# Query chunks, half key tiles and output rows laid out as contiguous pieces in an attention and top-k kernel

## The chip, the core and the metric

One core of a Trainium2 chip runs the kernel; the other seven are idle. The metric is device time in microseconds of one execution, the median of several runs, lower is better. The engines are TensorE (PE, with its weight loads as PEld), VectorE (DVE), ScalarE (ACT), GpSimd (POOL) and SyncE (SP), which issues every load, store and DMA transpose of the main loop.

## What is computed

For each of four batches: keys and values are the 4 x 4 mean of `kv`, projected with `w_sr`; 12288 queries of 128 channels attend to 768 keys; then the 128 rows with the highest score `x @ w_gate` pass through a small MLP and are written back.

```python
kv_pool = kv.reshape(B, H // r, r, W // r, r, C).mean(axis=(2, 4))
k = v = kv_pool.reshape(B, -1, C) @ w_sr
s = scale * (q @ k.transpose(0, 2, 1))
a = np.exp(s - s.max(-1, keepdims=True)); a /= a.sum(-1, keepdims=True) + 1e-09
x = a @ v
top_idx = np.argpartition(-scores[b], capacity)[:capacity]     # scores = x @ w_gate
out[b, top_idx] = x[b, top_idx] + sigmoid(scores[top_idx])[:, None] * (relu(xe @ w1) @ w2)
```

## The kernel before

The work is cut into 192 blocks of 256 queries (`BLK`), 48 for each batch. For block i TensorE makes 2 x 128 x 768 scores in PSUM (`S`, three products of split operands), VectorE takes the row maximum (`s_max`, tile `m`, one instruction in each block), ScalarE the exponential (`exp`, tile `am`). The weights are split into an fp16 high part (ScalarE) and a bf16 low part (GpSimd, for most of it), tile `hl`, and `turn` transposes each part with one DMA transpose (`at<-hl`, 128 x 11 x 128 of two bytes). Four blocks later (`LAG`) `AV` multiplies the transposed weights with the values into `o_two`. VectorE divides, and `finish` collects `GROUP` blocks in tile `x` before a store goes to `out`.

Queries come in chunks of `CHUNK` columns, 128 channels on the partitions. `load_q` (L138) loads half a chunk of 2048 at a time, which is 1024 columns or 512 KB, into one of two buffers; `split_q` (L356) reads it on ScalarE and GpSimd two blocks at a time. In the array `in_q` (L848) one channel's data of all batches and chunks follow each other, so a channel's rows lie 4 x 12288 x 4 B = 192 KiB apart and each load reads 128 pieces of 4 KB. Keys are loaded by `load_kv` (L126) in six tiles for each batch, most of them as two halves of 512 KB, for the first batch at the start and for the next batch while the blocks of this one run (`next_keys`, L298). `in_kv` (L849) has the same 192 KiB between channels. Pooling of the next keys runs on GpSimd. An output tile holds 2048 rows as 16 rows for each partition, of which a store (L476) writes eight: 4 KB out of every 8 KB.

The order on the four compute engines is the order of the code (`InOrder`). SP isn't held to that: its transfers are ordered by a scheduler, and an SP instruction that waits holds all that stand behind it. Transfers take eight semaphores in turn, so each also waits for the one eight before it.

Of the kernel before, what the change touches and what calls it, by code (L numbers as in the profile page):

```python
# [19 lines left out]
P = 128  # L20
B, N, C = 4, 12288, 128
HK, WK, R = 384, 32, 4
M = (HK // R) * (WK // R)
KT = M // P
TAPS = R * R
CHUNK = 2048
JPC = CHUNK // P
NCH = N // CHUNK
QT = 2
BLK = QT * P  # L30
NBLK = N // BLK
BPC = CHUNK // BLK
VC = C + 2
NCOL = N // P
CUT = 2 * M - P
GROUP = 4
OWN = 256
SHARE = CUT - OWN
ORDER = (2, 3, 4, 0, 1, 5)
# [32 lines left out]
def attention_topk_mlp(ctx, tc, a, outs, capacity):  # L72
    nc = tc.nc
# [4 lines left out]
    kvp = ctx.enter_context(tc.tile_pool(name="kvp", bufs=3))  # L78
    kvs = ctx.enter_context(tc.tile_pool(name="kvs", bufs=2))
    keys = ctx.enter_context(tc.tile_pool(name="keys", bufs=2))  # L80
    qp = ctx.enter_context(tc.tile_pool(name="qp", bufs=2))
    qs = ctx.enter_context(tc.tile_pool(name="qs", bufs=3))
    wk = ctx.enter_context(tc.tile_pool(name="wk", bufs=3))
    hlp = ctx.enter_context(tc.tile_pool(name="hlp", bufs=4))
# [41 lines left out]
    def load_kv(b, kc, parts=1, t=None):  # L126
        late = t is not None
        if not late:
            t = kvp.tile([P, 2, P // 2, TAPS], F32, name="kv_raw")
        n = 2 // abs(parts)  # L130
        for i in range(abs(parts)):
            if parts > 0 or late == (i > 0):
                nc.sync.dma_start(out=t[:, i * n:(i + 1) * n], in_=a["kv"][:, b, kc, i * n:(i + 1) * n])
        return t

    qraw = {}

    def load_q(b, ch, lo=0, hi=CHUNK):  # L138
        if (b, ch) not in qraw:
            qraw[b, ch] = qp.tile([P, CHUNK], F32, name="q_raw")  # L140
        nc.sync.dma_start(out=qraw[b, ch][:, lo:hi], in_=a["q"][:, b, ch, lo:hi])

    kvset = {}

# [77 lines left out]
    def first_keys():  # L222
# [3 lines left out]
        nc.sync.dma_start(out=cst, in_=a["cst"])  # L226
        raws += [load_kv(0, kc, 2) for kc in range(3, KT)]
        load_q(0, 0, 2 * BLK, CHUNK)
        split_q(0, 0)
        kv = kvset[0]  # L230
        for kc in range(KT):
# [124 lines left out]
    def split_q(b, blk):  # L356
        ch, h = divmod(blk, BPC)
        raw = qraw[b, ch][:, h * BLK:(h + 2) * BLK]
        qh = qs.tile([P, 2 * BLK], F32R, name="qh")
        ql = qs.tile([P, 2 * BLK], BF16, name="ql")  # L360
        act.copy(qh, raw)
        pool.tensor_tensor(out=ql, in0=raw, in1=qh.bitcast(F32), op=ALU.subtract)
        for i in range(2):
            h = qh[:, i * BLK:(i + 1) * BLK]
            top = h.bitcast(BF16).rearrange("p (n h) -> p n h", h=2)[:, :, 1]
            qsplit[b, blk + i] = h, top, ql[:, i * BLK:(i + 1) * BLK]
# [96 lines left out]
    def finish(n):  # L463
        b, blk = blocks[n]
        o, rz = st[n]["o"], st[n]["rz"]
        if blk % GROUP == 0:
            xt_[b] = ob.tile([P, GROUP * QT, C], F32, name="x")
        x = xt_[b]
        if b not in scores:
            scores[b] = tk.tile([P, NCOL], F32, name="sc")  # L470
        if n < nb - 2:
            dve.tensor_tensor(out=scores[b][:, blk * QT:(blk + 1) * QT], in0=o[:, :, C + 1], in1=rz, op=ALU.mult)
        dve.tensor_tensor(out=x[:, (blk % GROUP) * QT:(blk % GROUP + 1) * QT], in0=o[:, :, 0:C], in1=rz.rearrange("p (j o) -> p j o", o=1).broadcast_to([P, QT, C]), op=ALU.mult)
        if blk % GROUP == GROUP - 1:
            ch, h = divmod(blk // GROUP, BPC // GROUP)
            nc.sync.dma_start(out=outs[b].rearrange("(h p j) d -> h p j d", p=P, j=JPC)[ch, :, h * GROUP * QT:(h + 1) * GROUP * QT], in_=x)  # L476
        del st[n]

    def topk(b):
# [189 lines left out]
    for i in range(nb):  # L669
        m = i - LAG + (i < TURN)  # L670
        old = m >= 0 and i != TURN
        b, blk = blocks[i]
        if blk % GROUP == 0 and i + BPC < nb:
            nb_, nblk = blocks[i + BPC]
            load_q(nb_, nblk // BPC, nblk % BPC * BLK, (nblk % BPC + GROUP) * BLK)
        if blk == 0 and b + 1 < B:
            start(prep, next_keys(b + 1))
        if i:
# [183 lines left out]
```

## Time and profile before

| | |
|---|---|
| runs of the kernel before | 980.07, 983.41, 985.01 us, median 983.41 us |
| the profiled execution | 981.31 us; its span 979.5 us |
| granted TensorE clock, mean | 0.971 |
| moved by DMA | 217.61 MB, mean 222 GB/s |
| transposes, query loads, half key tiles, stores | 384, 46, 36, 48 |

The span is the time from the first to the last instruction; the execution's own time is 1.8 us longer. All times in rows are microseconds from the span's start, if nothing else is said. A busy TensorE isn't TensorE at its best, since matmuls overlap; a DMA share over 1 means that packets of one engine overlap.

### The profile page before, as it was taken

The page shows a single profiled execution, that of the slowest core. Times are in us where ns is not written, and L with a number is a line of the kernel's source. Part 1 is how long each engine was busy: PE and PEld are TensorE (multiplying, and loading weights), DVE is VectorE, ACT ScalarE, POOL GpSimd, SP SyncE. Part 2 cuts the span into 40 slices and gives each one's busy share as a digit, 9 for nine tenths or more (in the row PEclk, how much of TensorE's full clock was granted, in tenths as well). Part 3 has the DMA queues.
Part 4 walks back from the last instruction along what each step waited for, and adds up shares of the span by engine and source line. Part 5 has one row for each costly group of instructions (what it writes and reads, how often), then busy time and mean ns, then how long its engine had stood idle before and what let it go on. Part 6 is the DMA issues. An engine that isn't in the chain of part 4 may idle for free.

```text
span 979.5 us, 26075 instructions
## 1 busy us (share of the span) xinstructions
PE 895.3 (91%) x9797; PEld 718.0 (73%) x9971; DVE 752.7 (77%) x2120; ACT 748.0 (76%) x1361; POOL 691.3 (71%) x487
## 2 busy tenths in 40 slices
PE   4899898999999899899999989999999999999954
PEld 3577777777777787787777767877787877877743
DVE  6767676676788788688777768888868888888874
ACT  3688687787988788788888768888888888888700
POOL 2587677776787878788778778888767766667500
PEclk9999999999999999999999999999999999999966
DMA  9899999999999999999999999999989999999910
GB/s 360 225 237 218 226 239 249 239 229 232 253 225 224 239 263 229 234 249 248 224 213 233 216 248 263 223 227 220 226 172 229 226 241 222 231 216 189 206 37 6
DMA packets 574687, 217.61 MB, mean 222 GB/s; under 512 B 555360, under 2 KB 556512, under 8 KB 573792
## 3 DMA queue, kind: packets, MB, share of 16 engines
q1 hardware_dynamic: 574304, 215.41, 104.8%
q8 instruction: 78, 1.28, 0.6%
q0 software_dynamic: 256, 0.52, 0.2%
q14 instruction: 49, 0.40, 0.1%
HBM read 52.04 MB, written 25.43 MB: 79 GB/s over the span
## 4 chain that ended last, share of the span: by engine, by line
PE 54%; DMA 13%; issue 10%; DVE 9%; POOL 7%; ACT 6%; POOLq 0%; SPq 0%; DVEq 0%; ACTq 0%
PE s L57 29%; PE o_two L57 25%; DMA at<-hl 12%; DVE m L57 3%; ACT am L57 3%; POOL hl L57 3%; POOL ql L57 2%; POOL kv_sum L57 2%; ACT hl L57 2%; DVE junk L57 1%; DMA kv_raw<-in_kv 1%; DVE pooled L57 1%; ACT s L57 1%; DVE hl L57 0%; DVE mg L57 0%
## 5 line engine op out<-in xcount | busy, mean ns | idle before, releaser
L57 POOL TENSOR_TENSOR hl<-am,hl 128x1152 bf16<-128x1152 f32 x191 | 453.9, 2377 | 216.4 <-ACT hl L57 109.2
L57 PE MATMUL o_two<-vx,at 128*128 128x130 f16 x6804 | 438.6, 221 | 26.8 <-DMA at<-hl 26.2
L57 PEld LDWEIGHTS <-at 128*128 128x128 f16 (+1 forms) x6912 | 402.5, 97 | 82.5 <-issue 46.5
L57 DVE TENSOR_REDUCE m<-s 128x2 f32<-128x1536 f32 x192 | 337.3, 1757 | 112.8 <-PE s L57 112.4
L57 ACT ACTIVATE am<-s,m 128x512 f32<-128x512 f32 (+1 forms) x384 | 306.3, 798 | 100.8 <-DVE m L57 99.0
L57 PE MATMUL s<-kh,qh 128*128 128x512 f32 (+1 forms) x768 | 362.6, 474 | 0.0
L57 PE MATMUL s<-kb,ql 128*128 128x256 bf16 (+1 forms) x705 | 227.6, 323 | 7.2 <-issue 0.7
L57 ACT CAST hl<-am 128x1152 f16<-128x1152 f32 x192 | 225.3, 1173 | 0.0
L57 PE MATMUL s<-kl,qh 128*128 128x256 bf16 (+1 forms) x657 | 213.0, 324 | 1.3 <-DVE mg L57 0.5
L57 PEld LDWEIGHTS s<-kh,qh 128*128 128x128 f32 x768 | 146.9, 191 | 50.5 <-issue 1.7
L57 POOL TENSOR_TENSOR ql<-q_raw,qh 128x512 bf16<-128x512 f32 x96 | 122.7, 1278 | 6.2 <-ACT qh L57 6.2
L57 PEld LDWEIGHTS <-qh 128*128 128x128 bf16 x768 | 83.5, 109 | 22.7 <-issue 5.4
L57 ACT ACTIVATE s<-s,m 128x256 f32<-128x256 f32 x192 | 86.0, 448 | 6.3
L57 PEld LDWEIGHTS <-ql 128*128 128x128 bf16 x768 | 75.9, 99 | 5.9 <-issue 1.8
L57 DVE TENSOR_TENSOR hl<-s,hl 128x256 bf16<-128x256 f32 x192 | 79.5, 414 | 0.1
L57 DVE TENSOR_TENSOR x<-o_two,rz 128x256 f32<-128x256 f32 x189 | 78.3, 414 | 0.0
L57 ACT CAST at<-s 128x128 f16<-128x128 f32 x192 | 50.9, 265 | 34.2 <-PE s L57 33.9
L57 DVE TENSOR_TENSOR at<-s,at 128x128 bf16<-128x128 f32 x192 | 54.8, 285 | 22.5 <-ACT at L57 19.1
L57 ACT CAST hl<-s 128x256 f16<-128x256 f32 x191 | 71.1, 372 | 0.0
L57 PE MATMUL s<-cst,am 128*128 128x128 f32 x192 | 61.2, 319 | 8.1 <-ACT am L57 7.7
L57 PEld LDWEIGHTS s<-cst,am 128*128 128x128 f32 x192 | 26.9, 140 | 54.9 <-ACT am L57 52.8
L57 DVE TENSOR_SCALAR rz<-o_two,sg 128x2 f32<-128x2 f32 x189 | 40.9, 216 | 29.0 <-PE o_two L57 27.9
(171 smaller groups left out, 632.4 us busy)
## 6 DMA issues: line engine op xcount, KB each, us to landing
out<-x SPq DMA_DIRECT2D x48, 512.0 KB, 3.8
q_raw<-in_q SPq DMA_DIRECT2D x46, 512.0 KB, 5.1
kv_raw<-in_kv SPq DMA_DIRECT2D x36, 512.0 KB, 4.9
kv_raw<-in_kv SPq DMA_DIRECT2D x6, 1024.0 KB, 9.2
at<-hl SPq DMA_TRANSPOSE x384, 4.3
w<-in_w SPq DMA_DIRECT2D x2, 512.0 KB, 8.6
q_raw<-in_q SPq DMA_DIRECT2D x1, 768.0 KB, 7.1
cst<-in_cst SPq DMA_DIRECT2D x1, 320.0 KB, 9.7
```

The source lines that it names most:

```text
L57: r = f(*args, **kwargs)
```

## The change

Both input arrays get another order in memory: `in_q` is now batch, chunk, channel, column with `CHUNK` = 1024, and `in_kv` is batch, tile, half, channel, key, so what one load reads (1024 columns of 128 channels, or half a key tile) is one stretch of 512 KB, still 4 KB for each partition. A whole key tile is read as two such stretches, with pieces of 4 KB where 8 KB stood. The chunk of 1024 queries is 128 partitions of eight rows each, so the four blocks of one store are one stretch of 512 KB too. There are four query buffers of half the size, and one load fills one of them; in the code it stands eight blocks (`AHEAD`) before its use, as before. At the start the second part of the first chunk and the second chunk are two loads. The numbers that turn a position in a tile into a row of `out` follow `CHUNK`.

```diff
-CHUNK = 2048
+CHUNK = 1024
...
-GROUP = 4
+GROUP = BPC
+AHEAD = 2 * BPC
...
-    qp = ctx.enter_context(tc.tile_pool(name="qp", bufs=2))
+    qp = ctx.enter_context(tc.tile_pool(name="qp", bufs=4))
...
-                nc.sync.dma_start(out=t[:, i * n:(i + 1) * n], in_=a["kv"][:, b, kc, i * n:(i + 1) * n])
+                nc.sync.dma_start(out=t[:, i * n:(i + 1) * n], in_=a["kv"][b, kc, i * n:(i + 1) * n].rearrange("h c k t -> c h k t"))
...
-        nc.sync.dma_start(out=qraw[b, ch][:, lo:hi], in_=a["q"][:, b, ch, lo:hi])
+        nc.sync.dma_start(out=qraw[b, ch][:, lo:hi], in_=a["q"][b, ch, :, lo:hi])
...
         load_q(0, 0, 2 * BLK, CHUNK)
+        load_q(0, 1)
...
-            ch, h = divmod(blk // GROUP, BPC // GROUP)
-            nc.sync.dma_start(out=outs[b].rearrange("(h p j) d -> h p j d", p=P, j=JPC)[ch, :, h * GROUP * QT:(h + 1) * GROUP * QT], in_=x)
+            nc.sync.dma_start(out=outs[b].rearrange("(h p j) d -> h p j d", p=P, j=JPC)[blk // GROUP], in_=x)
...
-        if blk % GROUP == 0 and i + BPC < nb:
-            nb_, nblk = blocks[i + BPC]
-            load_q(nb_, nblk // BPC, nblk % BPC * BLK, (nblk % BPC + GROUP) * BLK)
+        if blk % GROUP == 0 and i + AHEAD < nb:
+            nb_, nblk = blocks[i + AHEAD]
+            load_q(nb_, nblk // BPC)
...
-        "q": np.ascontiguousarray(q.reshape(B, NCH, P, JPC, C).transpose(4, 0, 1, 3, 2).reshape(C, B, NCH, CHUNK)),
-        "kv": np.ascontiguousarray(kv.reshape(B, KT, 2, HK // R // KT // 2, R, WK // R, R, C).transpose(7, 0, 1, 2, 3, 5, 4, 6).reshape(C, B, KT, 2, P // 2, TAPS)),
+        "q": np.ascontiguousarray(q.reshape(B, NCH, P, JPC, C).transpose(0, 1, 4, 3, 2).reshape(B, NCH, C, CHUNK)),
+        "kv": np.ascontiguousarray(kv.reshape(B, KT, 2, HK // R // KT // 2, R, WK // R, R, C).transpose(0, 1, 2, 7, 3, 5, 4, 6).reshape(B, KT, 2, C, P // 2, TAPS)),
```

The sequences of TensorE, VectorE, ScalarE and GpSimd stay what they were. SP's changes in where the loads stand. Its first place is in the third batch, in the trace of before from 548 to 575 us. Names ending in a number are one buffer's use; an `x2` behind a transpose is a block's high and low part. Before:

```order
L133 DMA kv_raw_9491<-in_kv 128x1024
L476 DMA out_2<-x_8508 128x1024
L440 DMA_TRANSPOSE at_8727<-hl_8726 128x11x128 x2
L141 DMA q_raw_9086<-in_q 128x1024
L440 DMA_TRANSPOSE at_8810<-hl_8809 128x11x128 x2
L141 DMA q_raw_9086<-in_q 128x1024
L440 DMA_TRANSPOSE at_8888<-hl_8887 128x11x128
L133 DMA kv_raw_9491<-in_kv 128x1024
L440 DMA_TRANSPOSE at_8888<-hl_8887 128x11x128
L440 DMA_TRANSPOSE at_8973<-hl_8972 128x11x128 x2
L476 DMA out_2<-x_8828 128x1024
```

And the same place on SP now:

```order
L134 DMA kv_raw_9508<-in_kv 128x1024
L477 DMA out_2<-x_8523 128x1024
L442 DMA_TRANSPOSE at_8742<-hl_8741 128x11x128 x2
L142 DMA q_raw_9424<-in_q 128x1024
L442 DMA_TRANSPOSE at_8826<-hl_8825 128x11x128 x2
L134 DMA kv_raw_9508<-in_kv 128x1024
L442 DMA_TRANSPOSE at_8904<-hl_8903 128x11x128 x2
L442 DMA_TRANSPOSE at_8989<-hl_8988 128x11x128 x2
L477 DMA out_2<-x_8844 128x1024
L442 DMA_TRANSPOSE at_9071<-hl_9070 128x11x128 x2
L142 DMA q_raw_9746<-in_q 128x1024
```

The second query load has moved from beside the first to four blocks behind it, and no longer stands ahead of the half key tile. The second place on SP is in the last batch, where no keys are loaded. Before:

```order
L476 DMA out_3<-x_12401 128x1024
L440 DMA_TRANSPOSE at_12616<-hl_12615 128x11x128 x2
L141 DMA q_raw_12957<-in_q 128x1024 x2
L440 DMA_TRANSPOSE at_12698<-hl_12697 128x11x128 x2
L440 DMA_TRANSPOSE at_12775<-hl_12774 128x11x128 x2
```

Now:

```order
L477 DMA out_3<-x_12422 128x1024
L442 DMA_TRANSPOSE at_12637<-hl_12636 128x11x128 x2
L142 DMA q_raw_13295<-in_q 128x1024
L442 DMA_TRANSPOSE at_12720<-hl_12719 128x11x128 x2
L442 DMA_TRANSPOSE at_12797<-hl_12796 128x11x128 x2
L442 DMA_TRANSPOSE at_12877<-hl_12876 128x11x128 x2
L477 DMA out_3<-x_12738 128x1024
L442 DMA_TRANSPOSE at_12953<-hl_12952 128x11x128 x2
L142 DMA q_raw_13604<-in_q 128x1024
```

Two loads behind each other, once in eight blocks, have become one load in every four. SP's wait on GpSimd, which stood at the first of the two, now stands at each from the sixth chunk on.

## Rows read from the trace of the kernel before

**Rows 1.** The page: busy time, share of the span and instructions of each engine, and the mean busy share of the DMA engines in 40 slices (tenths).

```profile
PE 895.3 (91%) x9797; PEld 718.0 (73%) x9971; DVE 752.7 (77%) x2120; ACT 748.0 (76%) x1361; POOL 691.3 (71%) x487
...
DMA  9899999999999999999999999999989999999910
```

**Rows 2.** The chain of waits from 848 to 880 us, in order of time: start, us, what. `s` are scores, `o_two` the products with values.

```profile
852.65 2.23 PE s L57 x12
854.88 1.05 PE o_two L57 x18
...
855.93 1.05 PE o_two L57 x18
856.98 2.23 PE s L57 x12
```

**Rows 3.** Instructions on tile `m`, the row maximum: duration in ns min/median/max, first and last start.

```profile
L57 DVE TENSOR_REDUCE m<-s x192: 1742/1757/1759, 25.6 to 921.4; 128x2 f32<-128x1536 f32 x192
```

**Rows 4.** What TensorE waited for from 25.6 to 925.7 us, its matmuls in the first row and its weight loads in the second: us in total, times, longest.

```profile
PE o_two L57 <- DMA at<-hl: 26.2, 30, 3.8
...
PEld L57 <- DMA at<-hl: 35.2, 35, 3.9
```

**Rows 5.** What TensorE's matmuls waited for from 746 to 925.7 us, all rows.

```profile
PE s L57 <- ACT am L57: 1.0, 2, 0.6
PE o_two L57 <- DVE x L57: 0.4, 2, 0.3
PE s L57 <- DVE hl L57: 0.3, 1, 0.3
```

**Rows 6.** Stretches of the first, third and last batch: start to end, length, busy time of PE, PEld, DVE, ACT and POOL (instructions), granted clock, DMA share, GB/s. The stretches below have the same columns.

```profile
25.60:260.00 234.40, 213.96 (x2292) 168.57 (x2328) 163.64 (x361) 181.45 (x326) 173.88 (x122) 0.98 1.13 233
...
485.10:712.10 227.00, 216.54 (x2412) 174.32 (x2455) 181.51 (x510) 187.61 (x344) 180.83 (x131) 0.99 1.11 228
712.10:925.70 213.60, 210.31 (x2389) 168.70 (x2431) 175.25 (x484) 182.23 (x328) 147.00 (x82) 1.00 1.05 214
```

**Rows 7.** The first and the last of five such stretches (the others begin at 223.4, 339.4 and 397.5 us).

```profile
110.70:114.10 3.40, 3.40 (x25) 2.78 (x24) 0.88 (x4) 0.00 (x0) 1.56 (x2) 0.51 1.30 228
...
571.50:574.90 3.40, 2.93 (x27) 2.88 (x28) 0.96 (x6) 0.00 (x0) 0.37 (x1) 0.51 1.17 330
```

**Rows 8.** TensorE in order of time ahead of those two stretches: start, us, instruction, and in brackets the idle time before it with what ended it.

```profile
109.15 0.86 PE L57 MATMUL o_two<-vx,at 128*128 128x130 f16 x12 [1.97 <-DMA at<-hl]
...
571.75 0.83 PE L57 MATMUL o_two<-vx,at 128*128 128x130 f16 x6 [3.75 <-DMA at<-hl]
```

**Rows 9.** DMA issues: count, KB each, median us from issue to landing.

```profile
q_raw<-in_q SPq DMA_DIRECT2D x46, 512.0 KB, 5.1
kv_raw<-in_kv SPq DMA_DIRECT2D x36, 512.0 KB, 4.9
...
at<-hl SPq DMA_TRANSPOSE x384, 4.3
```

**Rows 10.** Stretches through one query load that was issued at 136.4 us between transposes: the transposes ahead of it, its first and second microsecond, its end, the transposes behind it.

```profile
136.60:137.40 0.80, 0.75 (x8) 0.59 (x7) 0.42 (x4) 0.74 (x2) 0.80 (x2) 1.00 1.28 288
137.60:138.60 1.00, 1.00 (x10) 0.78 (x8) 0.59 (x2) 0.87 (x2) 0.76 (x1) 1.00 1.25 164
138.60:139.60 1.00, 1.00 (x16) 0.75 (x15) 0.51 (x1) 1.00 (x3) 0.00 (x0) 1.00 0.76 168
139.60:140.20 0.60, 0.60 (x14) 0.60 (x12) 0.60 (x1) 0.51 (x1) 0.01 (x1) 1.00 0.96 353
140.20:141.00 0.80, 0.80 (x18) 0.80 (x16) 0.80 (x2) 0.05 (x1) 0.80 (x1) 1.00 1.41 185
```

**Rows 11.** Stretches from a load's first byte until transposes run at their rate again: that query load alone, then two pairs of query loads; the last row is a store, first to last byte.

```profile
137.40:141.10 3.70, 3.70 (x48) 3.16 (x47) 2.79 (x5) 2.53 (x5) 1.88 (x2) 1.00 1.08 204
...
175.40:180.50 5.10, 5.02 (x55) 3.99 (x56) 3.90 (x10) 4.19 (x10) 5.01 (x6) 1.00 1.05 235
...
808.30:812.90 4.60, 4.55 (x56) 3.71 (x55) 4.15 (x13) 4.08 (x8) 2.65 (x2) 1.00 1.05 262
...
246.60:247.80 1.20, 1.20 (x23) 1.19 (x21) 1.20 (x1) 0.80 (x1) 1.20 (x2) 1.00 1.10 408
```

**Rows 12.** Stretches at the kernel's start, before any transpose: `w_sr` (64 KB, contiguous), the first query piece (2 KB for each channel), whole key tiles (8 KB pieces), half key tiles and query pieces.

```profile
2.00:2.20 0.20, 0.00 (x0) 0.00 (x0) 0.00 (x0) 0.02 (x1) 0.00 (x0) 1.00 0.56 159
2.20:2.80 0.60, 0.00 (x0) 0.00 (x0) 0.00 (x0) 0.22 (x1) 0.00 (x0) 1.00 0.81 119
4.00:9.00 5.00, 0.00 (x0) 0.00 (x0) 2.04 (x2) 0.59 (x1) 1.25 (x1) 1.00 0.99 406
12.00:20.00 8.00, 6.67 (x43) 5.83 (x44) 7.81 (x8) 2.61 (x9) 2.66 (x8) 1.00 1.02 407
```

**Rows 13.** SP in order of time: start, us that the issue took with its waits, instruction.

```profile
554.83 1.49 SPq L141 DMA_DIRECT2D q_raw<-in_q  x1
...
560.46 0.56 SPq L141 DMA_DIRECT2D q_raw<-in_q  x1
...
562.56 0.58 SPq L133 DMA_DIRECT2D kv_raw<-in_kv  x1
563.24 8.71 SPq L440 DMA_TRANSPOSE at<-hl  x3
```

**Rows 14.** What SP waited for at query loads: us in total, times, longest.

```profile
SPq L141 <- POOL ql L57: 4.1, 4, 1.7
...
SPq L141 <- POOL pooled L57: 2.6, 2, 1.5
```

## The prediction

> **What bounds the kernel now.** I read the page first: TensorE is busy 91% of the span and the DMA engines are at 0.9 or more in nearly every slice [rows 1]. Two resources are near their limit, so the question is which of them ends a block. In the chain of waits the late blocks show it: twelve score matmul records (2.23 us) and two groups of value products (1.05 us each) follow each other with nothing between, and a block starts every 4.33 us (852.65 to 856.98) [rows 2]. That is TensorE's floor. The row-maximum instruction runs once per block, first at 25.6 and last at 921.4 us [rows 3]: 895.8 us for 191 steps, where the floor is 191 x 4.33 = 827.0. So 68.8 us of the main loop are lost.
>
> Next I asked what TensorE waited for in the loop. The one large item that isn't its own issue or a short wait on ScalarE is the DMA transpose `at<-hl`: 26.2 us seen by the matmuls, 35.2 us seen by the weight loads, up to 3.9 us at once [rows 4]. In the last 180 us before the tail, where no keys are loaded, no DMA wait is left at all [rows 5]. The stretches say the same: the first batch has DMA share 1.13 and TensorE busy 213.96 of 234.40 us, the last 1.05 and 210.31 of 213.60 [rows 6]. A long wait costs a second time: just after five of them the granted clock is 0.50 to 0.51 for 3.4 us, which is 1.2 instead of 2.4 GHz, after a stretch in which TensorE sat idle [rows 7, 8]. Half of 5 x 3.4 us is 8.5 us. DMA therefore costs the loop 26.2 + 8.5 = 34.7 to 35.2 + 8.5 = 43.7 us; I take the middle, 39. The other 30 us have other causes (the start, short waits on ScalarE) and aren't touched.
>
> **Why transposes are late.** All transfers go through SP's queue in order. A transpose lands 4.3 us after its issue in the median, a query load 5.1, a half key tile 4.9 [rows 9]. The rate during one query load tells why: transposes before it move 288 GB/s, the first two microseconds of the load 164 and 168, its end 353, and the transposes that follow start at 185 [rows 10]. From its first byte until transposes run freely again the single load takes 3.7 us; two in a row take 4.6 to 5.1, so 2.3 to 2.6 each. A store of the same size moves 408 GB/s and takes 1.3 us [rows 11]. The same strided loads, streaming at the kernel's start with no transposes, reach 406 to 407 GB/s, or 524,288 B / 407 = 1.29 us for 512 KB [rows 12]. So the pieces 192 KiB apart aren't slow in a stream; their onset is. One pair of rows bears on the cause: the first transfer of all (`w_sr`, contiguous) moves 159 GB/s at a DMA share of 0.56, the strided query piece behind it 119 at a share of 0.81 [rows 12]. Per busy share that is 284 against 147 GB/s, although the contiguous one has pieces of only 512 B.
>
> Per four blocks (17.3 us at the floor) the engines owe: eight transposes of 128 x 1408 x 2 B = 360,448 B at 288 GB/s, 1.25 us each, 10.0; one store, 1.3; one query load, 2.3 to 2.6 as half of a pair; and in the first three batches one half key tile (12 in 48 blocks), 2.3 to 3.7. Together 15.9 to 17.6 us of 17.3 with keys, 13.6 to 13.9 without. The first waits and the second doesn't [rows 4, 5]: the queue is just full.
>
> **The change, part by part.** *Contiguous loads.* If the onset goes, a load costs between 1.29 us and what it costs now; I take 1.5, near the streaming rate, because the contiguous first transfer shows no slow onset. Four blocks then owe 10.0 + 1.3 + 1.5 + 1.5 = 14.3 us, near the last batch's 13.6 to 13.9, which has no DMA wait. Of 39 us I let 5 stay, for stages where keys and queries still come together, and none to all of it as the bounds. *Single query loads.* The order shows one load per eight transposes in place of two per sixteen, so around 549 to 572 us, where SP now issues query, query and key tile within 8 us and one transpose group then takes 8.71 us [rows 13], one of the three is gone. That only helps, by an amount that is inside the 39. *Waits.* Every query load from the sixth chunk on now waits for GpSimd to leave its buffer, where every second one did. Such waits cost SP 4.1 and 2.6 us in 4 and 2 places [rows 14]; twice that is 7 us more, with the transposes queued behind. A block's transposes are read four blocks later, so I cost it at nothing (0 to 2 us); without that slack it would be the 7 us. *Stores* already move at full rate [rows 11]: 0. *Key tiles loaded whole* go from pieces of 8 KB to 4 KB: 406 and 407 GB/s are the two rates, 0 [rows 12]. *The start*: the slow 0.6 us at 119 instead of 406 GB/s could give back 0.4 us [rows 12]; 0 to 0.4, left out. The order of the instructions on the four compute engines doesn't change.
>
> Sum: 39 - 5 = 34 us off the profiled execution (981.31 us, its span 979.5), so 947; off the median of the runs (983.41), 949. What is late next is TensorE itself, at its 4.33 us a block [rows 2].
>
> **The rivals.** *B: the layout doesn't matter, the onset stays.* For it: strided pieces stream at full rate [rows 12], so memory can serve them, and the onset may belong to any read behind transposes; no row shows a contiguous read there. Then pairs become singles, which shortens the bursts but pays the onset twice. I take the two as even: 983 us, 978 to 988. The Trainium skill, DMA: Bandwidth & Descriptors, section Latency and other measured facts, says that copies lose rate only when the rows of a tile lie 2 MiB or more apart, and keep it at 512 KiB; it advises contiguous tiles beyond. By that rule 192 KiB costs nothing and B is the outcome; the trace agrees for the stream and speaks against it for the onset, which the rule doesn't tell of.
>
> *D: slower.* Same mechanism, but the second onset outweighs the shorter bursts. A query load goes from 2.4 to 3.7 us; 36 of them lie in the three batches with keys, 47 us more DMA time. Today 72 loads there cost 1.0 to 2.4 us above streaming, about 120 us, and 39 of it reaches TensorE, a third. A third of 47 is 15 us, less some relief from the shorter bursts: 994 us. It decides at 2.4 us: a single contiguous load that holds the engines for longer makes the kernel slower, for less makes it faster.
>
> *The change does less than it says*: the onset shrinks to half. Loads at 2.2 us give 15.7 us per four blocks, below the 15.9 to 17.6 of now; two thirds of the 34 would still come, 961. I count it with the forecast.
>
> **How the numbers follow.** Forecast 0.68, at 949 (941 to 963: all 43 us gone to only half the onset gone). B 0.20 at 983. D 0.12 at 994. A measurement of this kernel can tell about 0.5% (4.9 us) from no change. Faster than that: the forecast and a little of B, 0.72. Within: most of B, some of D, 0.16. Slower: 0.12. The range 940 to 985 holds the forecast and more than half of B, about 0.8; the forecast's own range is 941 to 963.
>
> **What would show it.** Right: single loads that hold the engines for 1.3 to 2 us, at over 300 GB/s from the first microsecond; a landing time of query loads under 4.5 us; `at<-hl` waits of TensorE under 10 us where they were 26.2 and 35.2; no half-clock stretch after the first; the first three batches within 3% of the last one's pace. Wrong: the same 150 to 200 GB/s at onset (B or D), or DMA waits gone and their time back as waits on GpSimd or ScalarE.

## The result, and the profile after

The changed kernel takes 994.73 us (median of 6 runs, 991.79 to 1000.32), the kernel before in the same session 982.72 (6 runs, 976.43 to 986.55): ratio 1.0134, 95% interval 1.009 to 1.0177. It is slower by 12.0 us, where 34 us less were forecast. The profiled execution took 996.49 us, its span is 994.7. Three executions of the runs below (one of e6, two of e7) took over 1.5% longer than the fastest of the same kernel, 1003.06 to 1014.43 us, and are left out of the tables.

The page: TensorE's row and the busy share of the DMA engines. Both stand as in [rows 1].

```profile
PE 900.9 (91%) x9797; PEld 722.9 (73%) x9971; DVE 752.2 (76%) x2120; ACT 748.8 (75%) x1361; POOL 691.9 (70%) x487
...
DMA  9899999999999999999999999999999999999910
```

The row maximum, which answers to [rows 3]: it starts 1.0 us later, and its 191 steps take 936.8 - 26.6 = 910.2 us where they took 895.8. Nearly the whole loss lies in the loop.

```profile
L58 DVE TENSOR_REDUCE m<-s x192: 1743/1758/1760, 26.6 to 936.8; 128x2 f32<-128x1536 f32 x192
```

What TensorE's matmuls waited for from 26.6 to 941 us, then its weight loads (two answers of the same view). In [rows 4] the transposes stood at 26.2 and 35.2; now they cost 38.0 and 51.4, in more but shorter waits. One execution is a small sample here: e14 and e15 below run as fast as the kernel before and show 31.5 / 43.5 and 32.2 / 43.9.

```profile
PE o_two L58 <- DMA at<-hl: 38.0, 39, 2.7
PE s L58 <- ACT am L58: 6.5, 10, 3.1
...
PEld L58 <- DMA at<-hl: 51.4, 54, 2.8
```

The four batches (columns as in [rows 6]). The first three are 5.3, 4.3 and 4.7 us longer than before (239.70 against 234.40, 229.40 against the 225.1 from 260.0 to 485.1 us, 231.70 against 227.00); the last takes 213.60 as it did. Look at the last column too: 225 to 232 GB/s wherever keys are loaded, at a DMA share well over 1. The first row is the second batch before, which [rows 6] leave out.

```profile
260.00:485.10 225.10, 214.66 (x2381) 172.02 (x2424) 181.66 (x508) 186.20 (x341) 179.52 (x129) 0.98 1.17 240
...
26.60:266.30 239.70, 215.66 (x2292) 170.60 (x2328) 164.02 (x361) 181.72 (x326) 173.91 (x122) 0.97 1.13 228
266.30:495.70 229.40, 213.96 (x2376) 170.87 (x2418) 181.53 (x507) 186.51 (x340) 179.78 (x129) 0.99 1.15 232
495.70:727.40 231.70, 219.30 (x2410) 176.82 (x2457) 180.62 (x509) 187.67 (x344) 180.93 (x131) 0.98 1.15 225
727.40:941.00 213.60, 210.33 (x2388) 168.69 (x2431) 175.22 (x484) 182.31 (x328) 147.18 (x82) 1.00 1.08 214
```

The DMA issues, median landing time last. In [rows 9] queries stood at 5.1, half key tiles at 4.9 and transposes at 4.3; neither kind of load lands sooner, and transposes land later. The six whole key tiles do land sooner (7.4 us against 9.2), the stores later (4.5 against 3.8).

```profile
q_raw<-in_q SPq DMA_DIRECT2D x47, 512.0 KB, 5.1
kv_raw<-in_kv SPq DMA_DIRECT2D x36, 512.0 KB, 5.1
...
at<-hl SPq DMA_TRANSPOSE x384, 4.6
```

Stretches through one contiguous query load, as [rows 10] showed a strided one: transposes at 292 GB/s ahead of it, then 71 and 115 in its first two microseconds, 334 at its end. The slow onset is still there. The last row is one of seven stretches of the loop at clock 0.50, 1.2 GHz, each just behind a wait for transposes; before there were five [rows 7].

```profile
256.20:257.00 0.80, 0.80 (x7) 0.40 (x6) 0.52 (x4) 0.80 (x3) 0.00 (x0) 1.00 1.61 292
257.00:258.00 1.00, 1.00 (x20) 1.00 (x20) 0.89 (x1) 1.00 (x3) 0.00 (x0) 1.00 1.26 71
258.00:259.00 1.00, 1.00 (x21) 1.00 (x19) 1.00 (x2) 0.66 (x3) 0.82 (x1) 1.00 0.32 115
259.00:260.00 1.00, 1.00 (x8) 0.54 (x7) 0.93 (x5) 0.97 (x2) 1.00 (x1) 1.00 0.98 334
260.00:261.00 1.00, 1.00 (x10) 0.78 (x7) 0.76 (x3) 1.00 (x3) 1.00 (x2) 1.00 1.16 207
...
610.60:614.00 3.40, 3.18 (x20) 2.60 (x19) 1.46 (x8) 1.73 (x5) 0.17 (x1) 0.50 1.15 195
```

### The profile page after: what moved, and what is told of

It reads as the page before. It is cut to its first block, busy times and chain, and to the rows that moved or that the text cites. A ratio compares the mean times of both kernels' runs of the same rounds, so it can differ in the third digit from the quotient of the medians.

```text
span 994.7 us, 26096 instructions
## 1 busy us (share of the span) xinstructions
PE 900.9 (91%) x9797; PEld 722.9 (73%) x9971; DVE 752.2 (76%) x2120; ACT 748.8 (75%) x1361; POOL 691.9 (70%) x487
## 4 chain that ended last, share of the span: by engine, by line
PE 50%; DMA 18%; issue 9%; DVE 9%; POOL 6%; ACT 6%; POOLq 0%; SPq 0%; DVEq 0%; ACTq 0%
PE s L58 27%; PE o_two L58 23%; DMA at<-hl 17%; DVE m L58 4%; ACT am L58 3%; POOL hl L58 2%; POOL kv_sum L58 2%; POOL ql L58 2%; ACT hl L58 1%; DMA kv_raw<-in_kv 1%; DVE junk L58 1%; ACT s L58 1%; DVE pooled L58 0%; DVE idx L58 0%; DVE mg L58 0%
## 5 line engine op out<-in xcount | busy, mean ns | idle before, releaser
L58 PEld LDWEIGHTS <-at 128*128 128x128 f16 (+1 forms) x6912 | 403.4, 98 | 96.3 <-DMA at<-hl 51.4
L58 ACT ACTIVATE am<-s,m 128x512 f32<-128x512 f32 (+1 forms) x384 | 306.4, 798 | 99.4 <-DVE m L58 98.5
L58 PEld LDWEIGHTS s<-cst,am 128*128 128x128 f32 x192 | 26.9, 140 | 51.7 <-ACT am L58 49.6
```

What stands on the lines that cost most here:

```text
L58: r = f(*args, **kwargs)
```

## The experiments

Each table gives the median, its runs and the ratio to the kernel before, which ran beside it on the same chip (984.7 to 986.2 us in the five sessions). The at<-hl column holds the waits of matmuls / weight loads on the transposes in the one profiled execution of each; before it was 26.2 / 35.2. In the cuts of code, `...` stands for what is left out.

### Layout or single loads?

`e1_layout_only` takes the contiguous layout alone: query loads still come in pairs into two large buffers, rows are stored as before.

```
-... in_=a["q"][:, b, ch, lo:hi])
+... in_=a["q"][b, ch, h, :, lo - h * HALF:hi - h * HALF])
...
-... in_=a["kv"][:, b, kc, i * n:(i + 1) * n])
+... in_=a["kv"][b, kc, i * n:(i + 1) * n].rearrange("h c k t -> c h k t"))
...
```

> The kernel before with the new order in memory alone: query half chunks and half key tiles contiguous, still two buffers of 2048 columns, so two query loads stand together once in eight blocks; stores as before. Onset theory (the first microseconds of a load behind transposes are slow whatever the layout, and single loads pay it twice as often): 983 us, 978 to 988, TensorE's wait on the transposes 26 us as before. Layout theory (contiguous pieces 16 KiB apart for neighbouring engines are slower to start than pieces 192 KiB apart): 990 to 995, waits near the 38 us of the changed kernel.

`e2_single_only` keeps the strided layout and takes four half buffers, so that query loads come one by one.

```
-qp = ctx.enter_context(tc.tile_pool(name="qp", bufs=2))
+qp = ctx.enter_context(tc.tile_pool(name="qp", bufs=4))
...
-    qraw[b, ch] = qp.tile([P, CHUNK], F32, name="q_raw")
+    qraw[b, ch, h] = qp.tile([P, HALF], F32, name="q_raw")
...
```

> The kernel before with single loads alone: four buffers of 1024 columns, so one query load stands in every four blocks; order in memory strided as before, stores as before. Onset theory: 992 to 998 us, waits on the transposes near 38 us. Layout theory: 983 us, since nothing in memory moved; with shorter bursts perhaps 978.

`e4_after_paired` is the changed kernel with two chunks in one buffer again, so that its loads pair up; loads and stores stay contiguous.

```
-qp = ctx.enter_context(tc.tile_pool(name="qp", bufs=4))
+qp = ctx.enter_context(tc.tile_pool(name="qp", bufs=2))
...
-    qraw[b, ch] = qp.tile([P, CHUNK], F32, name="q_raw")
+    qraw[b, pair] = qp.tile([P, 2, CHUNK], F32, name="q_raw")
...
```

> The changed kernel (contiguous loads and stores) with two chunks in one buffer, so that its query loads stand in pairs again. Onset theory: back to 983 us, 978 to 988. Layout theory: stays at 990 to 995. A loss that came from contiguous stores: stays at 990 to 995 while the layout of the loads alone costs nothing.

| kernel | us | lowest to highest | ratio, interval | at<-hl |
|---|---|---|---|---|
| layout alone (e1) | 991.23 | 986.99 to 995.77 | 1.0053, 1.0029 to 1.0076 | 35.9 / 47.5 |
| single loads alone (e2) | 987.79 | 983.09 to 992.36 | 1.0019, 0.9988 to 1.005 | 31.9 / 44.9 |
| after, paired (e4) | 991.89 | 986.32 to 994.73 | 1.0062, 1.0033 to 1.009 | 35.5 / 46.9 |

Neither half of the change gains. The layout costs 0.3 to 0.8%, as the layout theory had said of e1 and e4. With strided loads it isn't shown that single loads cost anything by themselves, since the interval of e2 includes 1; its 987.8 us fit neither theory (992 to 998, or 983). On top of the contiguous layout they do seem to cost: e1 and e4, which keep the pairs, are at 1.0053 and 1.0062, the changed kernel at 1.0134, its interval (1.009 to 1.0177) above that of e1 and meeting that of e4 at its edge; they come from two sessions, so this is a hint. e4 and e1 agree, so no gain or loss from contiguous stores shows. The medians of e1 and e2 add up to 6.4 + 3.0 = 9.4 of the 12.0 us.

### What a load costs among transposes

`m1_onset` holds transfers alone, in rows of repetitions: four transposes of the kernel's size, then one transfer of 512 KB.

```
+for i in range(16):
+    turns(4)
+    t = ld.tile([P, HALF], F32, name=name)
+    nc.sync.dma_start(out=t, in_=what(i))
```

> No part of the reference is computed: only transfers on one queue, in sections of 64 transposes with sixteen 512 KB transfers among them. Transposes alone take 1.25 us each, 5.0 us for four. Onset theory: four transposes and one load take 8.0 to 8.7 us, strided and contiguous alike; eight and a pair 14.6 to 15.1; a 1 MB load costs one onset like a pair; a copy inside SBUF or a store has no onset, 6.3 us; a load right behind a store has less of it, because the reading side can run ahead while the store is written. Layout theory: strided and contiguous singles differ by over 0.5 us each.

SP in order of time (start, us of the issue, instruction): first and last issue of a row of strided loads, of contiguous ones (`whole`), of strided pairs behind eight transposes each, of copies from SBUF (`inside`), of stores, then 64 transposes with nothing between.

```profile
51.11 0.92 SPq L51 DMA_DIRECT2D strided<-in_qs  x1
...
163.13 0.90 SPq L51 DMA_DIRECT2D strided<-in_qs  x1
...
171.79 0.90 SPq L51 DMA_DIRECT2D whole<-in_qc  x1
...
300.42 0.92 SPq L51 DMA_DIRECT2D whole<-in_qc  x1
...
316.02 1.26 SPq L58 DMA_DIRECT2D strided<-in_qs  x2
...
434.98 1.23 SPq L58 DMA_DIRECT2D strided<-in_qs  x2
...
580.25 0.78 SPq L68 DMA_DIRECT2D inside<-src  x1
...
705.85 0.76 SPq L68 DMA_DIRECT2D inside<-src  x1
...
714.24 0.80 SPq L71 DMA_DIRECT2D out<-src  x1
...
840.68 0.81 SPq L71 DMA_DIRECT2D out<-src  x1
841.54 110.16 SPq L33 DMA_TRANSPOSE at<-hl  x64
```

A transpose takes 110.16 / 64 = 1.72 us, not the 1.25 us of the prediction. A repetition takes (163.13 - 51.11) / 13 = 8.62 us with a strided load, (300.42 - 171.79) / 15 = 8.58 with a contiguous one, (705.85 - 580.25) / 15 = 8.37 with a copy from SBUF, and (840.68 - 714.24) / 15 = 8.43 with a store. Less 4 x 1.72 = 6.88 that leaves 1.74, 1.70, 1.49 and 1.55 us. Strided pairs take (434.98 - 316.02) / 7 = 16.99 us a repetition, contiguous pairs 16.87: 1.6 us a load, so a pair saves 0.1 to 0.15 us on each. A load of 1 MB takes 3.3 us, as much as a pair, and a load right behind a store isn't cheaper (3.4 us for both).

Stretches through one contiguous load of m1 (length, busy time of VectorE and GpSimd, clock, DMA share, GB/s): the transposes ahead of it, its first two microseconds, the transposes behind it.

```profile
257.00:259.00 2.00, 0.00 (x0) 0.00 (x0) 1.00 1.11 211
259.00:260.00 1.00, 0.00 (x0) 0.00 (x0) 1.00 0.75 147
260.00:261.00 1.00, 0.00 (x0) 0.00 (x0) 1.00 0.85 283
262.00:264.00 2.00, 0.00 (x0) 0.00 (x0) 1.00 1.27 265
```

The onset is there too, but the transposes behind the load then move 265 GB/s where those ahead of it moved 211: part of what the onset loses comes back. So in a full queue the slow onset costs at most some 0.25 us over a copy from SBUF, which has none (355 GB/s from 640.5 to 641.5 us), and the layout makes no difference. The layout theory (over 0.5 us a load) is out, and of the onset theory the 1.25 us of a transpose and the 6.3 us for a repetition with a copy or a store.

Four blocks with a key load then owe 8 x 1.72 + 1.55 + 2 x 1.74 = 18.8 us, or 226 a batch. That is the 225.1 and 227.00 us that the second and third batch took before [rows 6]; the first took 234.40, 8 us more, which stays unexplained. Without keys it is 17.05, or 205, under TensorE's 209.4 (209.3 in the last batch, 712.1 to 921.4 us). Theory T, for the runs that follow: the 16 DMA engines are full in batches 0 to 2. The expectations below count with a rougher split of the same rows, 1.6 us for a transpose and 2.0 us for any transfer of 512 KB, which adds up to the same 18.8.

### One queue, or the engines behind it?

`e5_after_kv_on_act` and `e6_before_kv_on_act` issue the loop's key loads from ScalarE's queue, `e7_after_q_on_act` the query loads.

```
e5 and e6
-nc.sync.dma_start(out=t[:, i * n:(i + 1) * n], in_=a["kv"]...
+(nc.sync if b == 0 else act).dma_start(out=t[:, i * n:(i + 1) * n], in_=a["kv"]...
e7
-nc.sync.dma_start(out=qraw[b, ch][:, lo:hi], in_=a["q"]...
+(nc.sync if (b, ch) < (0, 2) else act).dma_start(out=qraw[b, ch][:, lo:hi], in_=a["q"]...
```

> The changed kernel with the key and value loads of the loop (36 half tiles and whole tiles of batches 1 to 3) issued by ACT, so that they leave SP's queue; layout, query loads, stores and transposes stay. Theory Q (one queue in order is the bound of batches 0 to 2): by the run with transfers alone, a transpose takes 1.6 us of SP's queue and a 512 KB transfer behind it 2.0 us, so four blocks need 8 x 1.6 + 3 x 2.0 = 18.8 us, against 17.45 us that four blocks of the last batch take; without the key load 8 x 1.6 + 2 x 2.0 = 16.8 us fit, the batches fall from 239.7, 229.4 and 231.7 us to 210 to 220 each, waits of the matmuls on at<-hl from 38 us to under 10, and the time to 930 to 955 us. Theory E (the 16 DMA engines themselves are the bound, whatever queue feeds them): the same bytes at the same price, 985 to 1000 us. Rival: the load on its own queue takes the engines from a transpose that is due, and the issue costs ACT time: 1000 to 1015 us.

> The kernel before with the key and value loads of the loop issued by ACT, all else as before (strided pieces, query loads in pairs). Theory Q: batches 0 to 2 from 234.5, 225.0 and 227.0 us to 210 to 220, time 930 to 950 us. Theory E: 978 to 988 us. If the layout costs the same with the keys on their own queue, this one is 3 to 8 us faster than the changed kernel with the same edit; if the layout only counts where the queue is full, the two are within 2 us.

> The changed kernel with the query loads issued by ACT (all but the first two chunks), key loads on SP's queue. Theory Q: the same room as with the keys moved, in batches 0 to 2: 930 to 955 us; the last batch stays at 209 us, since its queue had room already. Theory E: 985 to 1000 us.

| kernel | us | lowest to highest | ratio, interval |
|---|---|---|---|
| after, keys by ScalarE (e5) | 997.87 | 988.23 to 999.33 | 1.0101, 1.0039 to 1.0163 |
| before, keys by ScalarE (e6) | 997.71 | 991.07 to 999.63 | 1.0112, 1.0062 to 1.0163 |
| after, queries by ScalarE (e7) | two runs | 986.88 and 988.21 | none |

The DMA queues of e5 (packets, MB, share of 16 engines):

```profile
q1 hardware_dynamic: 570080, 196.53, 100.4%
q10 hardware_dynamic: 5136, 18.88, 7.0%
```

What its matmuls waited for from 25.6 to 935 us, the largest row:

```profile
PE o_two L58 <- DMA at<-hl: 36.6, 30, 3.8
```

The key loads (18.88 MB) went over a queue of their own, and TensorE still waits 36.6 us for transposes that stand in another. A single queue in order isn't what delays them: theory Q falls, and E, the engines, stands. Whether it is the engines themselves or the memory behind them that is full, these runs don't tell apart. e7 gave no interval; its two runs lie in theory E's range of 985 to 1000 us, far from the 930 to 955 of theory Q.

`m2_engines_or_queue` asks the same with transfers alone.

```
+turns(4)
...
+nc.scalar.dma_start(out=t, in_=strided(i))
...
+turns(2)
+loads(1, "strided1", strided, nc.sync)
...
+turns(2)
+loads(1, "whole1", whole, nc.sync)
```

> Transfers alone, nothing of the reference is computed: rows of 16 repetitions of four DMA transposes on SP with one strided 512 KB load on ACT's queue beside them; 48 transposes issued by SP and ACT in turn; 24 strided and 24 contiguous loads with no transposes; rows of two transposes and one load, strided and contiguous. Theory T (engines): four transposes with the load beside them take 8.4 to 8.6 us as in one queue; transposes from two queues 1.5 to 1.6 us each; loads alone 1.3 to 1.6 us; two transposes and a load 3.2 + 2.0 = 5.2 us in either layout. Theory Q (SP's issue sets the pace): 6.5 us with the load beside, and 1.25 us or less for each of the transposes from two queues. A dearer contiguous load would show in the loads alone or in the row with two transposes, by more than 0.05 us a load.

SP in order of time: 128 transposes, in whose first part ScalarE's queue brought 16 loads; the second and the last of the rows with two transposes and one load (strided, then the first and last contiguous one). The last line is the only wait of SP on a transfer in the first of these stretches (us, times, longest).

```profile
3.20 249.92 SPq L33 DMA_TRANSPOSE at<-hl  x128
...
545.75 0.52 SPq L69 DMA_DIRECT2D strided<-in_qs  x1
...
608.11 0.53 SPq L69 DMA_DIRECT2D strided<-in_qs  x1
...
613.11 0.58 SPq L69 DMA_DIRECT2D whole<-in_qc  x1
...
691.00 0.53 SPq L69 DMA_DIRECT2D whole<-in_qc  x1
...
SPq L33 <- DMA at<-hl: 5.8, 1, 5.8
```

At 1.72 us, 128 transposes take 220.2 us. Of the other 29.7 us SP stood 5.8 at the end, when ScalarE's own transposes had begun (248.29 us). That leaves 23.9 us: 1.5 us for each of the 16 loads of the other queue, or 1.3 if two loads that SP had issued itself just before (0.74 us) are counted with them. They cost nearly what they cost in line. The rows give (608.11 - 545.75) / 12 = 5.20 us strided and (691.00 - 613.11) / 15 = 5.19 contiguous, 1.76 and 1.75 us a load, so neither layout is dearer. Two of the rows planned don't bear: the scheduler put all 16 of ScalarE's loads at the start, so that no period could be read there, and mixed strided with contiguous loads in the rows without transposes. Nor does the row with transposes from two queues: SP waited 130.0 us there for transposes to land, and 48 of them took 164.7 us.

### Are the engines full?

`e9_after_no_keys` leaves the loop's key loads out, `e10_single_strided_twice` and `e11_after_twice` issue each query load twice.

```
e9
+    fixed = []
...
+        if b:
+            return fixed[0]
...
e10 and e11
...
-    ob = ctx.enter_context(tc.tile_pool(name="ob", bufs=3))
+    ob = ctx.enter_context(tc.tile_pool(name="ob", bufs=2))
+    qd = ctx.enter_context(tc.tile_pool(name="qd", bufs=1))
...
+            nc.sync.dma_start(out=qd.tile([P, hi - lo], F32, name="q_again"), in_=...)
```

> The changed kernel without the loads of key and value tiles for batches 1 to 3 (their sums read the last tile of batch 0 again, which leaves those loads out). Theory T (the 16 DMA engines are full in batches 0 to 2: 1.6 us for a transpose and 2.0 us for a transfer of 512 KB, so 96 x 1.6 + 36 x 2.0 = 225.6 us a batch, against 209.4 us of TensorE's pace): without the 12 key loads a batch needs 96 x 1.6 + 24 x 2.0 = 201.6 us, TensorE sets the pace, and batches 0 to 2 take 209 to 214 us as the last one does; time 925 to 940 us. Rival L (each load holds up the transposes behind it by itself, whatever else is moved): the 48 query loads keep more than half of the loss, batches of 218 to 224 us, time 955 to 970 us. Rival P (the loss is made by other work of the key tiles on PE, ACT and GpSimd): batches stay at 225 us or more, time above 975 us.

> The kernel before with single query loads (as e2_single_only), and every query load of the loop issued twice, the second time into a buffer that nobody reads (46 more strided loads of 512 KB; two store buffers in place of three make the room). Theory T: 12 x 2.0 = 24 us more in each of batches 0 to 2, and in the last one 10 x 2.0 + 201.6 - 209.4 = 12 us more: about 84 us more than e2_single_only, 1060 to 1080 us. Rival L (a load only costs when it comes just ahead of a transpose that is due): 10 to 40 us more, 1000 to 1030 us.

> The changed kernel with every query load of the loop issued twice in the same way (46 more contiguous loads); its SP instructions stand in the order of e10_single_strided_twice. Theory T with a dearer contiguous load: the changed kernel is 7 us over e2_single_only with some 84 loads in the loop, 0.08 us each; with 130 loads this one is 9 to 14 us over e10. If the layout has no price of its own and the 7 us came of how loads and transposes happened to meet: between 5 us less and 5 us more than e10.

| kernel | us | lowest to highest | ratio, interval | at<-hl |
|---|---|---|---|---|
| after, no key loads (e9) | 945.16 | 943.62 to 946.23 | 0.959, 0.9557 to 0.9623 | none |
| strided, twice (e10) | 1085.14 | 1081.74 to 1088.42 | 1.1014, 1.0967 to 1.1061 | 98.5 / 126.6 |
| after, twice (e11) | 1091.17 | 1086.54 to 1093.54 | 1.1064, 1.1016 to 1.1111 | 104.6 / 136.5 |

All that TensorE's matmuls waited for in the loop of e9 (26.7 to 884.6 us), then its batches:

```profile
PE s L58 <- ACT am L58: 7.2, 11, 3.1
PE s L58 <- ACT hl L58: 1.4, 1, 1.4
PE s L58 <- DVE mg L58: 0.5, 2, 0.2
PE s L58 <- DVE hl L58: 0.3, 1, 0.3
PE s L58 <- POOL ql L58: 0.3, 1, 0.3
PE o_two L58 <- DVE x L58: 0.2, 1, 0.2
```

```profile
26.70:242.40 215.70, 208.74 (x2293) 165.65 (x2329) 163.35 (x362) 181.20 (x326) 173.99 (x122) 0.99 1.08 212
242.40:457.20 214.80, 210.82 (x2380) 169.03 (x2423) 180.75 (x508) 186.12 (x340) 179.67 (x129) 1.00 1.12 222
457.20:675.20 218.00, 214.21 (x2412) 172.78 (x2456) 180.89 (x510) 187.39 (x344) 180.90 (x131) 1.00 1.13 219
675.20:884.60 209.40, 206.83 (x2336) 165.61 (x2379) 171.88 (x477) 178.68 (x322) 144.47 (x78) 1.00 1.08 214
```

With the key loads gone no DMA wait is left, though 48 contiguous single loads with their onset still stand among the transposes. That speaks against rival L, by which each load costs by itself, and against P: the key tiles' work on the other engines is all still there (instruction counts as in the changed kernel). The time, 945.2 us, is 5 us over theory T's range, since the first three batches take 215 to 218 us and not 209 to 214: TensorE is busy for 209 to 214 us of each.

The 46 added loads of e10 cost 1085.1 - 987.8 = 97 us over e2, 2.1 us each, where theory T had said 84 (1060 to 1080 us), and far over the 10 to 40 of rival L. At 1.74 us of the engines each they are 80 us; part of the rest may be time at the lower clock (0.946 granted over the span, e2 0.975), which wasn't tested. e11 lies 6.0 us over e10, less than the 9 to 14 us of a dearer load and a little more than the 5 us of no price at all; the two intervals overlap, so this pair doesn't decide.

### What is left of the layout

`e8_kv_contiguous` and `e12_q_contiguous` take one half of e1's diff each. `e13_kv_whole_tile` keeps a whole key tile contiguous, in pieces of 8 KB; `e14_strided_pitch` adds 4 KB to the strided rows' pitch.

```
e13
-... in_=a["kv"][:, b, kc, i * n:(i + 1) * n])
+... in_=a["kv"][b, kc, :, i * n:(i + 1) * n])
...
e14
...
-"q": ... .reshape(C, B, NCH, CHUNK)),
+"q": np.pad(... .reshape(C, B * N), ((0, 0), (0, 1024))),
...
```

> The kernel before with the contiguous layout for the key half tiles alone; the query chunks stay strided and in pairs. The layout of both costs 6.5 us (ratio 1.0053). If every load of the contiguous layout pays the same, the keys' share is 36 of 84 loads: 2.5 to 3.5 us more than before (986.5 to 989). If the key tiles alone are the cause (whole tile from two pieces of 4 KB a partition in place of one of 8 KB, and more load on batches 0 to 2): 5 to 8 us more. If the queries alone are: within 1 us of before.

> The kernel before with the contiguous layout for the query halves alone, still loaded in pairs; the keys stay strided. Keys alone cost 5.3 us (e8_kv_contiguous), both 6.4 us (e1_layout_only). If the prices add, the queries alone cost 0 to 2 us (985 to 988); if each contiguous load costs the same, 48 loads give 3 to 4 us.

> The kernel before with each whole key tile contiguous (8 KB a partition in one piece, as before, so that the whole tile that opens a batch stays one row of 128 pieces; a half tile is 4 KB pieces at a pitch of 8 KB). Theory W (the split of the whole tile into 4 KB pieces costs it): within 1.5 us of before. Theory A (addresses close together cost it): 4 to 6 us more than before, as e8.

> The kernel before with 4 KB added to the pitch of the strided rows of queries and keys (196 KB in place of 192 KB a row); nothing else changes. If the layout before is neutral, within 1.5 us of before. If the pitch of 192 KB is a lucky one and any other addresses cost 3 us or more, the price of the contiguous layout is one of addresses.

| kernel | us | lowest to highest | ratio, interval | at<-hl |
|---|---|---|---|---|
| keys contiguous (e8) | 989.95 | 985.95 to 992.4 | 1.0042, 1.0022 to 1.0063 | 34.6 / 49.6 |
| queries contiguous (e12) | 989.25 | 984.86 to 996.35 | 1.0038, 1.0014 to 1.0061 | 31.2 / 42.2 |
| key tile of 8 KB pieces (e13) | 989.87 | 982.78 to 995.3 | 1.004, 1.0017 to 1.0063 | 30.0 / 43.5 |
| strided, other pitch (e14) | 985.72 | 981.05 to 987.68 | 0.9983, 0.9964 to 1.0002 | 31.5 / 43.5 |

Each contiguous form costs 0.1 to 0.6%; another strided pitch costs nothing. So it isn't the split of a whole tile into smaller pieces (theory W), nor a lucky pitch. The prices don't add: 0.42 and 0.38% apart, 0.53% together, which all their intervals allow.

`m3_mix_of_four_blocks` puts both layouts into the whole mix, with no compute engine at work.

```
+turns(2)
+nc.sync.dma_start(out=outs[...], in_=src...)
+turns(2)
+for k in range(2):
+    ...
+    nc.sync.dma_start(out=t, in_=what(2 * i + k))
+    turns(2)
```

> Transfers alone, nothing of the reference is computed: 12 times eight transposes, one store and two strided loads, 12 times the same with contiguous loads, and both once more. Theory T: 8 x 1.63 to 1.72 + 3 x 1.9 to 2.1 = 18.7 to 20.0 us for each, as the four-block groups with a key load take in the kernel. If the price of the contiguous layout is in the transfers once stores are among them, its rows are 0.15 us or more longer than the strided ones (two loads of some 0.08 us each); if it comes of how the loads meet the compute engines' needs, they differ by less than 0.1 us.

SP in order of time, stores alone: an early one of the row with strided loads, the first of the row with contiguous loads, the first of either row once more, and one near the end.

```profile
50.04 0.79 SPq L62 DMA_DIRECT2D out<-src  x1
...
257.13 0.80 SPq L62 DMA_DIRECT2D out<-src  x1
...
480.91 0.78 SPq L62 DMA_DIRECT2D out<-src  x1
...
706.16 0.79 SPq L62 DMA_DIRECT2D out<-src  x1
...
911.49 0.85 SPq L62 DMA_DIRECT2D out<-src  x1
```

Strided: 207.09 / 11 = 18.83 and 225.25 / 12 = 18.77 us a group. Contiguous: 223.78 / 12 = 18.65 and 205.33 / 11 = 18.67. The sum of 18.8 us is met, and groups with contiguous loads are 0.1 us shorter, not longer. The price that the layout has in the kernel isn't in these transfers taken alone; their loads all read queries, and a key tile was not among them.

### Two variants that might have gained

`e15_spread_halves` loads the second half of a key tile later; `e16_q_one_large` loads eight blocks of queries at once.

```
e15
-                if h == 3 and kc + 1 < KT:
+                if h == 5 and kc + 1 < KT:
e16
-        if blk % GROUP == 0 and i + BPC < nb:
+        if blk % BPC == 0 and i + BPC < nb:
...
-            load_q(nb_, nblk // BPC, nblk % BPC * BLK, (nblk % BPC + GROUP) * BLK)
+            load_q(nb_, nblk // BPC)
```

> The kernel before with the second half of a key tile loaded two steps of GpSimd's sums later (after the sixth in place of the fourth), so that the two halves of a tile lie some five blocks apart in place of three. Theory T (engines full on average): the total of the work is the same, 0 to 3 us less from fewer pile-ups. If pile-ups are most of the loss: 8 to 15 us less. If the tile is then late for the sums: more than before.

> The kernel before with each query chunk of eight blocks in one load of 1 MB (128 pieces of 8 KB in place of two loads of 128 pieces of 4 KB). Theory T with a price by bytes: the same time, within 3 us of before. If half the pieces cost the engines less: 1 MB at 3.5 us in place of 4.0 saves 0.5 x 24 = 12 us at most in batches 0 to 2, 975 to 983 us. If one load of 1 MB holds up the transposes behind it for longer than two of 512 KB: 3 to 10 us more.

e15: 985.63 us (979.44 to 988.84), ratio 0.9996, 0.9973 to 1.0019: no difference, as full engines let one expect. e16: 989.77 us (986.76 to 994.95), ratio 1.0061, 1.0035 to 1.0087: half the pieces buy nothing, and in the kernel one load of 1 MB is worse than two of 512 KB, although m1 shows one price for both (3.3 and 3.2 us; its 1 MB came in pieces of 4 KB). No variant that computes everything beat the kernel before by more than its interval.

## Why the prediction was wrong

**What held.** TensorE waits for transposes, only where keys are loaded, and DMA costs the loop some 39 us. e9 took the key loads away: no DMA wait is left, its loop (row maximum from 26.7 to 884.5 us) is 857.8 us, 38.0 shorter than before and 30.8 over the floor, and its median lies 985.5 - 945.2 = 40.4 us under the kernel before. It was made from the changed kernel, so this holds if the layout costs nothing where no DMA wait is left; that wasn't run. The prediction named the right loss. SP's waits on GpSimd at query loads, which it put at nothing, didn't grow either: 6.8 us where they were 7.1.

**The step that failed** is the one that the 34 us hang on: "If the onset goes, a load costs between 1.29 us and what it costs now; I take 1.5". The onset didn't go, and it wasn't what a load costs. Contiguous loads keep it (71 and 115 GB/s in the load shown), and their landing time stayed at 5.1 us, where under 4.5 was the sign of being right. In a full queue a contiguous load takes 1.70 us and a strided one 1.74 (m1), not 1.5 against 2.3 to 3.7. The 3.7 us for which a single load "holds the engines" [rows 11] are for the most part not lost: at 204 GB/s they move 755 KB, of which the load is 524, and the transposes behind a load move faster for a while (m1). To price a load by its low rate was the error; there was next to nothing to save. The hint from `w_sr` [rows 12] was one transfer with nothing ahead of it.

**A second term was mis-sized**, in the sum of what four blocks owe: "eight transposes ... at 288 GB/s, 1.25 us each, 10.0". The 288 GB/s came from 0.8 us of [rows 10]. In a long row a transpose takes 1.72 us (m1), eight 13.8. The real sum is 18.8 us, not 15.9 to 17.6, and the queue isn't "just full" at 17.3 but 1.5 us over in every group with a key load. Even with loads at the 1.5 us of the forecast and stores at 1.3 it would have been 13.8 + 1.3 + 3.0 = 18.1, still too much. The rows shown could have cast doubt on it: four blocks move 8 x 360,448 + 3 x 524,288 B = 4.46 MB, which in 15.9 to 17.6 us would be 253 to 280 GB/s, and no batch moves more than 240 ([rows 6], and 260.0 to 485.1 us), at a DMA share over 1.

**Rival B** said that the layout is neutral. For the transfers it is: 8.58 against 8.62, 5.19 against 5.20 us. The rule of the Trainium skill (DMA: Bandwidth & Descriptors, Latency and other measured facts), that rows of a tile lose rate only at far wider pitches than 192 KiB, agrees with these rows, and with e14. For the kernel it isn't, by 0.3 to 0.8% (e1), and its 983 us didn't come.

**Rival D** named 994, and 994.7 came, which is largely luck. Its 11 us were to come of a second onset in single loads, 2.4 us that become 3.7. Such a price exists but is a tenth of that: 1.74 us single against 1.6 in a pair (m1), or some 36 x 0.13 = 5 us as an estimate. e2 shows 0.19% (-0.12 to 0.5%), and the step from e1 and e4 to the changed kernel 5 us or so. The rest came with the layout, whose single load takes no longer than a strided one.

**The other steps.** Stores at 0: e4 agrees with e1. Key tiles in smaller pieces at 0: e13, which keeps the 8 KB, shows no lower cost than e8. Of single loads it said "That only helps": no run shows that it did. The start came 1.0 us later in the trace, not 0.4 earlier; e14, whose loads are strided as before, starts its row maximum 1.1 us later too, so this is no mark of the change.

**What stays open** is why the contiguous layout costs some 3 to 7 us in the kernel. It did so in e1, e4, e8, e12 and e13; it isn't the pairing, the stores, the size of a key tile's pieces or the pitch, and isn't in the transfers as far as m1, m2 and m3 can show. What is left is how the loads meet the compute engines' work. Two records bear on it. m3 moves 239 GB/s with contiguous loads at a DMA share of 1.10, the changed kernel 228, 232 and 225 at 1.13 to 1.15 in its first three batches (before 233, 240 and 228): the same transfers move more slowly in the kernel than alone, and why no run shows. And e16, in the old layout, lost as much (0.6%) by larger loads alone, which m1 prices like a pair. Batches 0 to 2 run with the engines at their limit, so that small shifts may decide which transpose is late; that this is the cause was only argued.

## What to carry to other kernels

Before an edit is priced, add up the bytes that the DMA engines move per turn of the loop, and check that the priced sum doesn't ask for a higher rate than any long busy stretch shows; a rate read in one microsecond isn't a price. Price a transfer by a row of them run alone, as m1 and m3 did. Where the engines are full, layout, pairing, another queue and the size of pieces gave nothing here or cost a little; only taking bytes away (e9) gave time back. Leaving the suspected transfers out is a cheap first experiment: it shows at once what they cost and whether anything else can give it back.

## What the hardware showed unexpectedly

- A transpose of 128 x 1408 elements of 2 bytes within SBUF takes 1.72 us in a long row (360,448 B / 1.72 us = 210 GB/s), as long as a plain transfer of 512 KB among transposes (1.5 to 1.75 us).
- A load from HBM behind transposes starts slowly, strided or contiguous (71 and 115 GB/s, then 334, in the kernel; 147, then 283, in m1), and costs only 0.2 to 0.25 us more in a full queue than a copy from SBUF (1.70 and 1.74 against 1.49 us). The transposes behind it move 265 GB/s for a while, those ahead of it 211.
- Loads on a queue of their own cost the transposes nearly as much as in the same queue: some 1.3 to 1.5 us each in m2 against 1.74, and e5 is no faster.
